# The first batch's second layer by seven products: right-hand sums made where the weights first stand, and one addition of the Fourier fold ahead of a subtraction

## The chip, the cores and the metric

The kernel runs on one core of one Trainium2 chip. The metric is the time of one execution on the device in microseconds (us); lower is better. All engines of the core (TensorE, VectorE, ScalarE, GpSimd, and SyncE, which issues most transfers) run their own queues of instructions in order and wait for each other by semaphores.

## The reference

Four batches of 8 heads of attention over 768 positions with 64 channels a head. A query sees a local window (distance under 16) and 24 block keys (the maximum of each 32 keys, with the blocks' mean values and log 32 added to the score). The heads are put side by side, x has 768 x 512 for each batch, and then:

```
X = np.fft.fft(x, axis=1)
X = np.fft.fft(X, axis=2)
mixed = np.real(X).astype(np.float32)
u = x + mixed
un = (u - mu) / np.sqrt(var + 1e-06)
ch = np.maximum(un @ w_ch1, 0.0) @ w_ch2
return (u + ch).astype(np.float32)
```

w_ch1 is 512 x 2048 and w_ch2 2048 x 512. Both come to the kernel as float64 and are turned into float32 on the chip.

## The kernel before

One program works through the four batches: attention of a batch, its Fourier transform as matrix products on folded halves (sums and differences of mirrored rows and columns, so that fewer products are needed), the layer norm, and the two layers. All products are float32 on TensorE. The order on each engine is the order in which a scheduler takes the Python program; `tc.issue_after(mark)` keeps a piece of work behind a marked instruction, and generators are driven in turn, so that the next batch's attention stands between the products of this batch's layers.

The layers are cut in two halves of the hidden channels, c = 0 and c = 1, four tiles of 256 hidden channels each (j, called weight tile 0 to 7). For a batch b the work runs: first layer of half 0 (`gen_hidden(b, 0)`), second layer of half 0 (`gen_out(b, 0)`), first layer of half 1, and then the second layer of half 1 beside the next batch's Fourier transform.

Products go by a scheme of seven in place of eight: a 2 x 2 block product needs seven products of sums of blocks (`A` blocks and left sums S1, S2, S3, S4; `B` blocks and right sums T1, T2, T3, T4). Each weight tile has seven parts: `_left_sums` or `_right_sums` makes parts 1 to 6 out of four blocks. T3 stands in the place of B12, so B12 is lost when T3 is made. Row tiles t (128 positions each) come in pairs i and i + 3; a pair's outcome is put together in three banks X, Y and Z of PSUM with a joining addition (`join`) after each product or two. PSUM gives four banks to this work (`bank`, a pool in turn) and four to the attention.

The weights of batch 0 are converted on the way (`convert`): raw words are loaded by SyncE (`load_raw`), VectorE masks exponent and mantissa (L1171, L1184), ScalarE does two steps (L1172, L1185), VectorE combines (L1187, L1189) and multiplies (through `tt`, whose additions and products all are recorded at L582). `gen_weights` goes through `plan`, a list of which weight tile is made when (first-layer tiles as (1, j), second-layer tiles as (2, j)), and each piece stands behind a stage's mark. A made tile is stored to DRAM (`dw1`, `dw2`) for the later batches, with its sums; the four second-layer tiles of half 0 were stored with their four blocks alone, batch 1 loaded these, made the sums between its first-layer products (`some_sums`) and stored them for batches 2 and 3.

In batch 0, half 0, the second layer goes without the seven products: six row tiles, each by eight plain products of 512 columns, L1730:

```
for n, j in enumerate(js):
    for hf in range(2):
        nc.tensor.matmul(ps, h[:, n, hf, P * t:P * (t + 1)], wt[2, b, j][:, 2 * hf:2 * hf + 2, :],
```

While they run, VectorE makes the weight tiles 3 of the second layer and 4, 5 and 6 of the first, and the attention of batch 1 goes on.

The fold of batch 0 (`mirror_halves`, `fold_channels`) runs on VectorE between the attention and the first transform (L1333): a mirror step makes sums and differences of mirrored columns (`zw`), then a channel step joins the two halves of the columns into `fg`.

Of the kernel before, what the change touches and what calls it, by code (L numbers as in the profile page):

```python
# [480 lines left out]
B11, T3, B21, B22, T1, T2, T4 = range(7)  # L481
A21, B12 = S3, T3
# [14 lines left out]
def _main_program(ctx, tc, q, k, v, moe_w_ch1, moe_w_ch2, out):  # L497
# [6 lines left out]
    NST = S // P  # L504
# [9 lines left out]
    HT = NST // 2  # L514
    HD = DM // 2
    NJ = NIT // 2
    NC = 4
# [63 lines left out]
    def tt(out, in0, in1, op):  # L581
        return nc.vector.tensor_tensor(out=out, in0=in0, in1=in1, op=op).ins  # L582
# [285 lines left out]
    def first_attention():  # L868

        x = x_of[0] = bpool.tile([P, NST, DM], FP, tag="x", bufs=2, name="x_0")  # L870
        fold = bpool.tile([P, 7, 2, S2], FP, tag="u", name="fold_0").rearrange("p a k n -> p (a k n)")
        wt["fold"] = split_fold(0, fold)
        turned = turned_to(0)
        for n in (1, 0):
            for e in range(2):
                turn(0, turned[0], n, e)
        for n in (1, 0):
            place(turned, n, 0, nc.scalar.copy)
            place(turned, n, 1, nc.vector.tensor_copy)
        key_maxima(0)  # L880
        load(0, 2)
        load_values(0, 1)
        load(0, 3)
        load_values(0, 2)
        ps, spread = {}, {}
        for g in range(-1, NP - 1):
            a, n = g + 1, g + 2
            ends = n == NP
            first = score_banks(a, 0)
            ps[a] = apool.tile([P, 2, NQ, QB], FP, tag="p", name=f"p_0_{a}")  # L890
            i = n - 1 if ends else g
            if i >= 0 and i not in spread:
                spread[i] = add_parts(i)
            wide_scores(a, 0, first)
            exponentials(ps[a], 0, first)
            if ends:
                spread_sums(n - 1, nc.scalar.copy, *spread[n - 1])
                mirror_halves(0, 0)
            elif g >= 0:
                spread_sums(g, nc.vector.tensor_copy, *spread[g])  # L900
            masks(ps[a], 0)
            second = score_banks(a, 1)
            if not ends:
                turned = turned_to(n)
                for i in ((1, 0), (1, 1), (0, 0), (0, 1))[:3 + (g < 0)]:
                    turn(n, turned[0], *i)
                place(turned, 1, 0, nc.scalar.copy)
                place(turned, 1, 1, nc.vector.tensor_copy if g < 0 else nc.scalar.copy)
                place(turned, 0, 0, nc.scalar.copy)
                if g < 0:  # L910
                    place(turned, 0, 1, nc.vector.tensor_copy)
                key_maxima(n % 2)
            wide_scores(a, 1, second)
            exponentials(ps[a], 1, second)
            masks(ps[a], 1)
            if g >= 0 and not ends:
                turn(n, turned[0], 0, 1)
                if g == 1:
                    spread[2] = add_parts(2)
                place(turned, 0, 1, nc.scalar.copy)  # L920
            if g >= 0:
                wide_values(0, g, ps[g], x)
            if g == 1:
                spread_sums(2, nc.scalar.copy, *spread[2])
            if g == 0:
                load_values(0, 3)
                load(1, 0)
                get_tables(0, lambda: load_raw(1))
                load_raw(2)
                block_sums(1, 0)  # L930
                load(1, 1)
                load_raw(4)
                fetch(out=sel, in_=dr["sel"].ap())
                fetch(out=near, in_=dr["near"].ap().rearrange("p (h i) c -> p h i c", h=2))
                fetch(out=half_of, in_=dr["half"].ap())
                fetch(out=mirror, in_=dr["mirror"].ap())
            for par in range(2 if g == 1 else 0):
                fold_sequence(par, 0, 2)
        mirror_halves(1, 0)
        fold_sequence(0, 2, 3)  # L940
        wide_values(0, NP - 1, ps[NP - 1], x)
        fold_sequence(1, 2, 3)
        load_values(1, 0)
        keep_busy(3, ps[NP - 1][:, 0].rearrange("p n c -> p (n c)"))
        nc.gpsimd.memset(zqs[0], 0.0)
        fold_sequence(0, 3, NP)
        mirror_halves(0, 1)
        fold_channels(0)
        fold_sequence(1, 3, NP)
        mirror_halves(1, 1)  # L950
        fold_channels(1)
# [3 lines left out]
        x, c = x_of[0], slice(P * g0, P * g1)  # L955
        tt(early[par][:, :, c], x[:, 0:HT, c], x[:, HT:NST, c], SUB if par else ADD)

    def mirror_halves(par, hi):

        Q, o = DM // 4, HD * hi  # L960
        sd, zw = early[par], wt["fold"][:, par]
        up, down = sd[:, :, o + 1:o + Q], sd[:, :, o + HD - 1:o + Q:-1]
        tt(zw[:, :, o + 1:o + Q], up, down, ADD)
        tt(zw[:, :, o + Q + 1:o + HD], up, down, SUB)

    def fold_channels(par):

        Q = DM // 4
        sd, zw, fg = early[par], wt["fold"][:, par], wt["fold"][:, 2 - 2 * par]
        edge = lambda c: (sd[:, :, c:c + 1], sd[:, :, HD + c:HD + c + 1])  # L970
        tt(fg[:, :, 0:1], *edge(0), ADD)
        tt(zqs[0][:, par, :, 0:1], *edge(Q), ADD)
        nc.gpsimd.memset(fg[:, :, Q:Q + 1], 0.0)
        plus, minus = (slice(o + 1, o + Q) for o in (0, Q))
        over, under = (slice(HD + o + 1, HD + o + Q) for o in (0, Q))
        tt(fg[:, :, plus], zw[:, :, plus], zw[:, :, over], ADD)
        tt(fg[:, :, minus], zw[:, :, minus], zw[:, :, under], ADD)
        tt(fg[:, :, HD:HD + 1], *edge(0), SUB)
        tt(fg[:, :, DM - 1:DM], *edge(Q), SUB)
        tt(fg[:, :, HD + 1:HD + Q], zw[:, :, minus], zw[:, :, under], SUB)  # L980
        marks["fold", 0] = tt(fg[:, :, HD + Q:DM - 1], zw[:, :, plus], zw[:, :, over], SUB)
# [214 lines left out]
    def make(f, j):  # L1196


        if f == 1:
            w = bpool.tile([P, 7, 2, P], FP, tag="w1", bufs=3, name=f"w1_0_{j}")  # L1200
            wv, to = w.rearrange("p a k n -> p a (k n)"), dw1[j].rearrange("p a k n -> p a (k n)")
        else:
            w = wv = bpool.tile([P, 7, HD], FP, tag="w2", bufs=NC, name=f"w2_0_{j}")
            to = dw2[j]
        yield from convert(pieces.index((f, j, 0)) // 2, wv[:, 0:4].rearrange("p a n -> p (a n)"))
        if f == 1:
            _left_sums(tt, wv)
        elif j < NC:

            to, wv = to[:, 0:4], wv[:, 0:4]  # L1210
        else:
            _right_sums(tt, wv)
        yield
        stores.append((to, wv))
        if len(stores) > 2 or len(pieces) == len(raws):
            fetch(out=stores[0][0], in_=stores.pop(0)[1])
        wt[f, 0, j] = w
        yield
# [20 lines left out]
        fetch(out=w, in_=dw1[j])  # L1239
        wt[1, b, j] = w  # L1240

    to_sum = []

    def some_sums(n):
        with tc.issue_after(marks["dense"]):
            for f, a in to_sum[:n]:
                f(*a)
        del to_sum[:n]

    def get_w2(b, j):  # L1250
        w = bpool.tile([P, 7, HD], FP, tag="w2", bufs=NC, name=f"w2_{b}_{j}")
        if b == 0:
            return
        wt[2, b, j] = w
        if b == 1 and j < NC:
            marks["load"] = fetch(out=w[:, 0:4], in_=dw2[j][:, 0:4])
            _right_sums(lambda *a: to_sum.append((tt, a)), w)
            to_sum.append((fetch, (dw2[j][:, 1:7], w[:, 1:7])))
        else:
            marks["load"] = fetch(out=w, in_=dw2[j])  # L1260


    tables = {}
# [177 lines left out]
    def gen_hidden(b, c):  # L1441
# [3 lines left out]
        for j in js:  # L1445
# [25 lines left out]
            nc.scalar.copy(out=c11, in_=X)  # L1471
            product(Y, A12, B21, True, True)
            marks["dense"] = tt(c11, Y, c11, ADD)
            some_sums(3 if (b, c) == (1, 0) and j else 0)
            yield
            product(X, S2_, T2, False, False)
            nc.scalar.copy(out=c12, in_=X)
            product(Z, S1, T1, True, False)
            nc.scalar.copy(out=c22, in_=Z)
            relu(c11)  # L1480
            some_sums(3 if (b, c) == (1, 0) and j else 0)
            yield
            product(X, S3, T3, False, False)
            marks["dense"] = tt(c22, X, c22, ADD)
            product(Z, S4, B22, False, True)
            marks["dense"] = tt(c12, Z, c12, ADD)
            some_sums(3 if (b, c) == (1, 0) and j else 0)
            yield
            product(X, A22, T4, False, True)
            nc.scalar.activation(out=c21, in_=X, func=AF.Relu)  # L1490
            relu(c22)
            relu(c12)
            issued.add(("h", b, j))
            some_sums(3 if (b, c) == (1, 0) and j else 0)
            yield

    H2 = S2 // 2
# [223 lines left out]
    def gen_out(b, c):  # L1721
        x, h = x_of[b], wt["h", b]
        js = range(NC * c, NC * (c + 1))
        if (b, c) == (0, 0):

            for t in range(NST):
                ps = bank([P, DM], f"o_{b}_{c}_{t}")
                for n, j in enumerate(js):
                    for hf in range(2):
# [2 lines left out]
                    if n % 2 == 0:  # L1732
                        yield
                tt(x[:, t, :], ps, x[:, t, :], ADD)
            issued.add(("o", b, c))
            return
        for i in range(HT):
            t1, t2 = slice(P * i, P * (i + 1)), slice(S2 + P * i, S2 + P * (i + 1))
            left = {A11: h[:, :, 0, t1], A12: h[:, :, 1, t1], A22: h[:, :, 1, t2]}
            for s in (S1, S2_, S3, S4):  # L1740
# [206 lines left out]
```

## Time and profile before

| what | value |
|---|---|
| time, median of 3 runs | 784.36 us (783.70 to 786.31) |
| the profiled execution | 782.39 us, span 780.6 us |
| granted TensorE clock | 0.999 |
| TensorE busy | 766.1 us, 98% of the span, 6020 products |
| VectorE busy | 534.4 us, 68% |
| ScalarE busy | 249.4 us, 32% |
| plain products of the first second layer | 96, from 126.8 to 173.4 us |

The span is the time from the first instruction to the last in the profiled execution. An engine's queue is in order, so an instruction that waits holds all behind it. In the rows of the timeline the first two numbers are the start and the busy time, and a bracket gives the idle time ahead of it and who ended it.

### The profile page before, as it was taken

The numbers are of one execution on the slowest core, as the hardware profiler recorded it, in microseconds if no ns is written. First come the engines' busy times: TensorE is split into PE (matmuls) and PEld (weight loads), VectorE is DVE, ScalarE is ACT, GpSimd is POOL, SyncE is SP. The second block draws the span as 40 slices with busy tenths as digits, with TensorE's granted clock in tenths as the row PEclk, the third lists the DMA queues.
The fourth block names the chain that finished last, engine by engine and source line by source line (L and its number), as shares of the span: only waits on it lengthen the run. The fifth ranks groups of instructions, "written<-read, shape, count | busy, mean of one in ns | idle before, by whom it ended". The sixth has DMA issues, their size and how long they took to land.

```text
span 780.6 us, 14876 instructions
## 1 busy us (share of the span) xinstructions
PE 766.1 (98%) x6020; PEld 578.0 (74%) x6020; DVE 534.4 (68%) x1123; ACT 249.4 (32%) x579; POOL 74.7 (10%) x102
## 2 busy tenths in 40 slices
PE   8999899999999999999999999999999999999997
PEld 5778555446598866787578866688669889889886
DVE  5789998777888556652758544553576887766762
ACT  4765656326536022100236012200126124104300
POOL 1001000000000030201210020300030004101500
PEclk9999999999999999999999999999999999999999
DMA  9998979696855179986342169720624143204001
GB/s 203 259 240 163 217 253 302 178 280 175 245 141 157 37 214 219 248 124 182 128 166 96 55 209 197 200 81 1 255 63 143 41 181 143 95 1 188 1 29 57
DMA packets 135900, 120.35 MB, mean 154 GB/s; under 512 B 94512, under 2 KB 117392, under 8 KB 135824
## 3 DMA queue, kind: packets, MB, share of 16 engines
q1 hardware_dynamic: 134672, 117.05, 54.9%
q0 software_dynamic: 576, 2.10, 0.7%
q8 instruction: 49, 0.80, 0.5%
q10 hardware_dynamic: 576, 0.17, 0.1%
q14 instruction: 27, 0.22, 0.1%
HBM read 95.71 MB, written 23.59 MB: 153 GB/s over the span
## 4 chain that ended last, share of the span: by engine, by line
PE 81%; DVE 9%; DMA 5%; ACT 3%; issue 1%; SPq 1%; POOL 0%; DVEq 0%; ACTq 0%; POOLq 0%
PE ox L1753 18%; PE hx L1460 13%; PE oz L1753 9%; PE hz L1460 6%; PE o L1730 5%; PE oy L1753 4%; PE t L1633 4%; DMA words<-in_moe_w_ch_dram 3%; PE hy L1460 3%; PE y L1333 2%; PE f L1633 2%; PE mx L1292 2%; PE sc L810 2%; PE av L846 1%; DVE w L582 1%
## 5 line engine op out<-in xcount | busy, mean ns | idle before, releaser
L1460 PE MATMUL hx<-u,w 128*128 128x384 f32 x384 | 140.0, 492 | 0.5 <-ACT h L1471 0.3
L1460 PEld LDWEIGHTS hx<-u,w 128*128 128x128 f32 x384 | 70.9, 190 | 52.8 <-ACT p L817 3.7
L1753 PE MATMUL oz<-w,s 128*128 128x256 f32 x336 | 81.7, 380 | 0.0
L1753 PE MATMUL ox<-w,s 128*128 128x256 f32 x336 | 80.1, 380 | 0.2 <-DVE s L582 0.2
L1753 PE MATMUL ox<-w,h 128*128 128x256 f32 x336 | 79.6, 381 | 0.0
L1753 PEld LDWEIGHTS ox<-w,h 128*128 128x128 f32 x336 | 63.0, 190 | 10.7 <-issue 1.2
L1460 PE MATMUL hz<-u,w 128*128 128x384 f32 x192 | 70.4, 487 | 0.4 <-DVE u L582 0.4
L582 DVE TENSOR_TENSOR x<-ox,x 128x256 f32<-128x256 f32 x84 | 35.5, 423 | 51.2 <-PE ox L1753 50.8
L1753 PEld LDWEIGHTS ox<-w,s 128*128 128x128 f32 x336 | 63.0, 190 | 9.6 <-DVE s L582 0.6
L1753 PEld LDWEIGHTS oz<-w,s 128*128 128x128 f32 x336 | 63.2, 190 | 9.0 <-DVE x L582 0.4
L1460 PEld LDWEIGHTS hz<-u,w 128*128 128x128 f32 x192 | 36.2, 190 | 25.7 <-DVE u L582 1.0
L1471 ACT COPY h<-hx 128x384 f32<-128x384 f32 x24 | 11.5, 478 | 118.7 <-PE hx L1460 118.7
L1730 PE MATMUL o<-w,h 128*128 128x512 f32 x96 | 42.2, 595 | 0.9 <-DVE w L582 0.9
L1753 PE MATMUL oy<-w,h 128*128 128x256 f32 x168 | 40.7, 381 | 0.7 <-ACT h L1682 0.7
L1636 ACT COPY f<-t 128x192 f32<-128x192 f32 x52 | 15.8, 303 | 78.3 <-PE t L1633 78.1
L1612 POOL TENSOR_SCALAR h<-h 128x768 f32<-128x768 f32 x12 | 25.4, 2128 | 137.6 <-DVE h L1592 137.6
L585 POOL TENSOR_TENSOR vb<-vb 96x512 f32<-96x512 f32 (+2 forms) x20 | 20.4, 1024 | 182.5 <-DMA vb<-in_v_dram 115.8
L1460 PE MATMUL hy<-u,w 128*128 128x384 f32 x96 | 35.2, 488 | 1.5 <-DVE h L582 1.5
L582 DVE TENSOR_TENSOR x<-oz,x 128x256 f32<-128x256 f32 x42 | 17.8, 423 | 26.7 <-PE oz L1753 26.4
L1753 PEld LDWEIGHTS oy<-w,h 128*128 128x128 f32 x168 | 31.5, 190 | 5.9 <-ACT h L1682 1.5
L1730 PEld LDWEIGHTS o<-w,h 128*128 128x128 f32 x96 | 18.0, 190 | 23.8 <-issue 21.2
L1490 ACT ACTIVATE h<-hx 128x384 f32<-128x384 f32 x24 | 11.7, 489 | 62.2 <-PE hx L1460 62.2
(236 smaller groups left out, 1327.4 us busy)
## 6 DMA issues: line engine op xcount, KB each, us to landing
w<-dw SPq DMA_DIRECT2D x42, 896.0 KB, 5.8
words<-in_moe_w_ch_dram SPq DMA_DIRECT2D x32, 512.0 KB, 5.8
dw<-w SPq DMA_DIRECT2D x12, 896.0 KB, 7.8
vw<-in_v_dram SPq DMA_DIRECT2D x47, 192.0 KB, 5.6
out_dram<-x SPq DMA_DIRECT2D x23, 256.0 KB, 2.0
vb<-in_v_dram SPq DMA_DIRECT2D x24, 192.0 KB, 6.9
kn<-in_k_dram SPq DMA_DIRECT2D x9, 384.0 KB, 5.9
qn<-in_q_dram SPq DMA_DIRECT2D x9, 384.0 KB, 7.0
```

The source lines that it names most:

```text
L582: return nc.vector.tensor_tensor(out=out, in0=in0, in1=in1, op=op).ins
L585: return nc.gpsimd.tensor_tensor(out=out, in0=in0, in1=in1, op=op).ins
L810: ins = nc.tensor.matmul(ps[h][r:r + 64, i, :], kt[rows, o:o + 64], qt[rows, o:o + BLOCK], start=True, stop=True)
L1292: nc.tensor.matmul(out, y[:, g], table, start=False, stop=True, skip_group_check=True)
L1333: nc.tensor.matmul(y, fgs[b][par][:, st, P * g:P * (g + 1)], fs[par][:, g % 2, st, :], start=(st == 0), stop=(st == n - 1))
L1460: ins = nc.tensor.matmul(ps, w[:, a, kk, :], u[:, r, kk, :], start=start and kk == 0, stop=stop and kk == 1, skip_group_check=True)
L1490: nc.scalar.activation(out=c21, in_=X, func=AF.Relu)
L1612: nc.gpsimd.tensor_scalar(out=t, in0=t, scalar1=0.0, scalar2=None, op0=ALU.max)
L1633: marks["two"] = nc.tensor.matmul(o, left(j, a, m), rhs(r, m), start=m in (1, 5), stop=m in (2, 3, 4, 5, 7), skip_group_check=True).ins
L1636: nc.scalar.copy(out={1: f[:, 0], 6: f[:, 1], 7: g}[m], in_=t)
L1730: nc.tensor.matmul(ps, h[:, n, hf, P * t:P * (t + 1)], wt[2, b, j][:, 2 * hf:2 * hf + 2, :], start=(n, hf) == (0, 0), stop=(n, hf) == (NC ...
L1753: nc.tensor.matmul(ps, left[a][:, n, :], wt[2, b, j][:, r, :], start=start and n == 0, stop=stop and n == NC - 1, skip_group_check=True)
```

## The change

Four edits.

The second layer of batch 0, half 0: the row tiles 0 and 3 stay plain. The pairs of tiles 1 and 4, and 2 and 5, go by seven products of 256 columns, with four left sums (128 x 512) and seven joins (128 x 256) a pair. Ahead of tile 0 stand T1, T2 and T4 of weight tiles 0 and 1, ahead of tile 3 those of weight tiles 2 and 3; behind tile 3 stand the four T3 and the stores of parts 1 to 6.

The making of these four weight tiles stores part 0 alone (128 KB in place of 512). Batch 1 loads all seven parts (896 KB in place of 512), and its twelve sums and four stores of 768 KB go.

In the fold of batch 0, one mirror step is cut in two: its addition stays, its subtraction moves into `fold_channels(0)`, behind the first of the joining additions there.

```diff
-        mirror_halves(0, 1)
+        mirror_halves(0, 1, ADD)
         fold_channels(0)
...
         tt(fg[:, :, plus], zw[:, :, plus], zw[:, :, over], ADD)
+        if par == 0:
+            mirror_halves(0, 1, SUB)
         tt(fg[:, :, minus], zw[:, :, minus], zw[:, :, under], ADD)
...
-            to, wv = to[:, 0:4], wv[:, 0:4]
+            to, wv = to[:, 0:1], wv[:, 0:1]
...
-        if b == 1 and j < NC:
-            marks["load"] = fetch(out=w[:, 0:4], in_=dw2[j][:, 0:4])
-            _right_sums(lambda *a: to_sum.append((tt, a)), w)
-            to_sum.append((fetch, (dw2[j][:, 1:7], w[:, 1:7])))
-        else:
-            marks["load"] = fetch(out=w, in_=dw2[j])
+        marks["load"] = fetch(out=w, in_=dw2[j])
...
-            some_sums(3 if (b, c) == (1, 0) and j else 0)
...
-        if (b, c) == (0, 0):
-
-            for t in range(NST):
+        plain = (0, HT) if (b, c) == (0, 0) else ()
+        if plain:
+            for t in plain:
+                for j in js[0:2] if t == 0 else js[2:4]:
+                    w = wt[2, 0, j]
+                    tt(w[:, T1], w[:, B12], w[:, B11], SUB)
+                    tt(w[:, T2], w[:, B22], w[:, T1], SUB)
+                    tt(w[:, T4], w[:, B21], w[:, T2], SUB)
                 ps = bank([P, DM], f"o_{b}_{c}_{t}")
...
                 tt(x[:, t, :], ps, x[:, t, :], ADD)
-            issued.add(("o", b, c))
-            return
-        for i in range(HT):
+            for j in js:
+                w = wt[2, 0, j]
+                tt(w[:, T3], w[:, B22], w[:, B12], SUB)
+                fetch(out=dw2[j][:, 1:7], in_=w[:, 1:7])
+        for i in range(1 if plain else 0, HT):
```

What this moves on the engines. First TensorE, around the scores of batch 1's last pair of heads in the second layer of half 0. Names: `ss` are the scores against block keys, `o_0_4` and `o_0_5` the banks of plain row tiles 4 and 5, `hx` the next first layer. Before:

```order
L828 MATMUL ss_3_1779<-qt_3_1554,km_83 32x384 x4
L1730 MATMUL o_0_4_1721<-w_0_1_1382,h_0_1255 128x512 x2
L1730 MATMUL o_0_4_1721<-w_0_2_1415,h_0_1255 128x512 x2
L1730 MATMUL o_0_4_1721<-w_0_3_1504,h_0_1255 128x512 x2
L1730 MATMUL o_0_5_1796<-w_0_0_1250,h_0_1255 128x512 x2
L1730 MATMUL o_0_5_1796<-w_0_1_1382,h_0_1255 128x512 x2
L1730 MATMUL o_0_5_1796<-w_0_2_1415,h_0_1255 128x512 x2
L1730 MATMUL o_0_5_1796<-w_0_3_1504,h_0_1255 128x512 x2
L1460 MATMUL hx_4_1809<-u_816,w_0_4_1538 128x384 x2
```

Now, at the same scores (`ox_0_1` and `oz_0_1` are banks X and Z of pair 1, `ox_0_2` is X of pair 2, `qk` the transposes of the next head, `s_0_0_1` the left sums of pair 1):

```order
L828 MATMUL ss_3_1843<-qt_3_1554,km_83 32x384 x4
L710 MATMUL qk_0_0_1912<-ident,kn_0_1233 128x128 x3
L710 MATMUL qk_0_1_1918<-ident,kn_0_1233 128x128 x3
L710 MATMUL qk_0_0_1924<-ident,qn_0_1235 128x128 x3
L710 MATMUL qk_0_1_1930<-ident,qn_0_1235 128x128 x3
L834 MATMUL vs_3_1937<-vbs_1_1237,sel 128x64
L1746 MATMUL ox_0_2_1775<-w_0_0_1250,h_0_1255 128x256
L1746 MATMUL ox_0_1_1728<-w_0_0_1250,s_0_0_1_1721 128x256
L1746 MATMUL ox_0_1_1728<-w_0_1_1382,s_0_0_1_1721 128x256
```

The transposes stand ahead of the second layer's remaining products. The first product of pair 2 takes the bank that plain tile 3 had, so it waits for the join of tile 3; the next one adds to bank X of pair 1 again and waits for that bank's first join.

Then VectorE, at the end of the conversion of weight tile 6. Names: `w_0_6` is that tile, `words` the raw words, `x_145` batch 0's rows, `x_919` batch 1's, `rec` the attention's reciprocals. Before:

```order
L582 TENSOR_TENSOR w_0_6_1620<-w_0_6_1620,words 128x1024
L1171 TENSOR_SCALAR words<-words 128x1024
L582 TENSOR_TENSOR x_919<-av_2_1_1635,rec 128x2x3x64
L582 TENSOR_TENSOR w_0_6_1620<-w_0_6_1620 128x256
L582 TENSOR_TENSOR x_145<-o_0_1_1617,x_145 128x512
L582 TENSOR_TENSOR w_0_6_1620<-w_0_6_1620 128x2x256
L582 TENSOR_TENSOR x_145<-o_0_2_1700,x_145 128x512
L582 TENSOR_TENSOR w_0_6_1620<-w_0_6_1620 128x256
L582 TENSOR_TENSOR x_145<-o_0_3_1711,x_145 128x512
```

Now:

```order
L582 TENSOR_TENSOR w_0_6_1632<-w_0_6_1632,words 128x1024
L582 TENSOR_TENSOR x_919<-av_2_0_1646,rec 128x2x3x64
L856 RECIPROCAL rec<-av_2_1_1647 128x6
L582 TENSOR_TENSOR w_0_6_1632<-w_0_6_1632 128x256
L582 TENSOR_TENSOR x_919<-av_2_1_1647,rec 128x2x3x64
L582 TENSOR_TENSOR w_0_6_1632<-w_0_6_1632 128x2x256
L582 TENSOR_TENSOR x_145<-o_0_3_1629,x_145 128x512
L582 TENSOR_TENSOR w_0_6_1632<-w_0_6_1632 128x256
L582 TENSOR_TENSOR w_0_3_1504<-w_0_3_1504 128x256
L582 TENSOR_TENSOR x_145<-ox_0_1_1728,x_145 128x256
L582 TENSOR_TENSOR x_145<-oz_0_1_1730,x_145 128x256
L582 TENSOR_TENSOR x_145<-oy_0_1_1729,x_145 128x256
```

Where the joins of plain tiles 1, 2 and 3 stood between the last sums of weight tile 6, there now stand the join of plain tile 3, the T3 of weight tile 3 and the first joins of pair 1's X, Z and Y. The conversions of weight tiles 4, 5 and 6 stand ahead of them in both.

Last VectorE in the fold of batch 0, after the attention of the last heads. Before:

```order
L582 TENSOR_TENSOR wide<-x_145 128x3x128 x2
L582 TENSOR_TENSOR fold_146<-wide 128x3x127 x2
L582 TENSOR_TENSOR fold_146<-wide 128x3 x2
L582 TENSOR_TENSOR fold_146<-fold_146 128x3x127 x2
L582 TENSOR_TENSOR fold_146<-wide 128x3 x2
L582 TENSOR_TENSOR fold_146<-fold_146 128x3x127 x2
```

Now:

```order
L582 TENSOR_TENSOR wide<-x_145 128x3x128 x2
L582 TENSOR_TENSOR fold_146<-wide 128x3x127
L582 TENSOR_TENSOR fold_146<-wide 128x3 x2
L582 TENSOR_TENSOR fold_146<-fold_146 128x3x127
L582 TENSOR_TENSOR fold_146<-wide 128x3x127
L582 TENSOR_TENSOR fold_146<-fold_146 128x3x127
L582 TENSOR_TENSOR fold_146<-wide 128x3 x2
L582 TENSOR_TENSOR fold_146<-fold_146 128x3x127 x2
```

One operation of 128 x 3 x 127 from `wide` (the mirror subtraction) now stands behind the first `fold`-from-`fold` addition.

More of the change, by code (lines that the diff above doesn't have):

```diff
@@ L956, in fold_sequence, with mirror_halves @@
         tt(early[par][:, :, c], x[:, 0:HT, c], x[:, HT:NST, c], SUB if par else ADD)
-    def mirror_halves(par, hi):
+    def mirror_halves(par, hi, *ops):
         Q, o = DM // 4, HD * hi
@@ L962, in mirror_halves @@
         up, down = sd[:, :, o + 1:o + Q], sd[:, :, o + HD - 1:o + Q:-1]
-        tt(zw[:, :, o + 1:o + Q], up, down, ADD)
-        tt(zw[:, :, o + Q + 1:o + HD], up, down, SUB)
+        for op in ops or (ADD, SUB):
+            at = o + (Q if op is SUB else 0)
+            tt(zw[:, :, at + 1:at + Q], up, down, op)
     def fold_channels(par):
@@ L1240, in get_w1 @@
         wt[1, b, j] = w
[L1242 to L1248, printed above, removed]
     def get_w2(b, j):
@@ L1480, in gen_hidden @@
             relu(c11)
-            some_sums(3 if (b, c) == (1, 0) and j else 0)
             yield
@@ L1486, in gen_hidden @@
             marks["dense"] = tt(c12, Z, c12, ADD)
-            some_sums(3 if (b, c) == (1, 0) and j else 0)
             yield
@@ L1493, in gen_hidden @@
             issued.add(("h", b, j))
-            some_sums(3 if (b, c) == (1, 0) and j else 0)
             yield
```

## The prediction

> **What bounds the kernel now.** I read the page first: busy time of each engine, then the chain that ended last.
>
> ```profile
> PE 766.1 (98%) x6020; PEld 578.0 (74%) x6020; DVE 534.4 (68%) x1123; ACT 249.4 (32%) x579; POOL 74.7 (10%) x102
> ...
> PE 81%; DVE 9%; DMA 5%; ACT 3%; issue 1%; SPq 1%; POOL 0%; DVEq 0%; ACTq 0%; POOLq 0%
> ```
>
> TensorE is busy for 98% of the span and carries 81% of the chain. Work taken off it is worth its full time, if nothing new makes it wait. So I asked what it waits for: over the whole span (three of the rows), and after 174 us (first and last of five rows).
>
> ```profile
> PE o L1730 <- DVE w L582: 0.9, 1, 0.9
> PE mx L1374 <- ACT big L1338: 0.7, 1, 0.7
> PE y L1333 <- DVE fold L582: 0.6, 1, 0.6
> ```
> ```profile
> PE oy L1753 <- ACT h L1682: 0.7, 2, 0.3
> ...
> PE y L1333 <- PE oz L1753: 0.2, 1, 0.2
> ```
>
> After 174 us the five add up to 1.6 us: a delay given to TensorE before that is hardly won back later. Then the busy time of the engines by stage (columns PE, PEld, DVE, ACT, POOL, clock, DMA share, GB/s):
>
> ```profile
> 126.50:174.00 47.50, 46.60 (x311) 21.72 (x310) 35.72 (x49) 16.70 (x23) 0.00 (x0) 1.00 0.83 249
> 174.00:230.00 56.00, 55.30 (x312) 37.19 (x312) 47.68 (x77) 28.44 (x61) 0.74 (x1) 1.00 0.69 196
> ```
>
> The first row is the stage of the change, the first second layer: TensorE is full, VectorE has 11.8 us free. The timeline of TensorE in it:
>
> ```profile
> 126.75 6.17 PE L1730 MATMUL o<-w,h 128*128 128x512 f32 x14
> 133.83 6.28 PE L1730 MATMUL o<-w,h 128*128 128x512 f32 x14 [0.90 <-DVE w L582]
> 140.03 1.20 PE L846 MATMUL av<-vw,p 64*32 64x65 f32 x96
> 141.16 0.94 PE L851 MATMUL av<-vs,p 64*128 64x130 f32 x12
> 142.03 17.43 PE L1730 MATMUL o<-w,h 128*128 128x512 f32 x40
> 159.40 1.60 PE L810 MATMUL sc<-qt,kt 64*64 64x32 f32 x96
> 160.93 0.85 PE L828 MATMUL ss<-qt,km 64*32 64x384 f32 x8
> 161.71 12.29 PE L1730 MATMUL o<-w,h 128*128 128x512 f32 x28
> 173.83 1.45 PE L1460 MATMUL hx<-u,w 128*128 128x384 f32 x4
> ...
> 178.99 0.82 PE L710 MATMUL qk<-ident,kn 128*128 128x128 f32 x6
> ...
> 180.30 1.46 PE L1460 MATMUL hx<-u,w 128*128 128x384 f32 x4
> 181.59 0.33 PE L834 MATMUL vs<-vbs,sel 96*128 96x64 f32 x2
> ```
>
> And VectorE's (an instruction's pitch is the distance to the next start):
>
> ```profile
> 135.85 0.69 DVE L582 TENSOR_TENSOR x<-o,x 128x512 f32<-128x512 f32 x1 [2.08 <-PE o L1730]
> 136.46 0.68 DVE L1171 TENSOR_SCALAR words<-words 128x1024 int32<-128x1024 int32 x1
> 137.06 0.69 DVE L1184 TENSOR_SCALAR w<-words 128x1024 int32<-128x1024 int32 x1
> 142.13 0.27 DVE L856 RECIPROCAL rec<-av 128x6 f32<-128x6 f32 x2 [4.39 <-PE av L851]
> 142.32 1.19 DVE L1187 SCALAR_TENSOR_TENSOR words<-words 128x1024 int32<-128x1024 int32 x1
> 143.42 1.22 DVE L1189 SCALAR_TENSOR_TENSOR w<-words,w 128x1024 f32<-128x1024 uint32 x1
> ...
> 159.03 0.40 DVE L582 TENSOR_TENSOR w<-w 128x256 f32<-128x256 f32 x1
> 159.36 0.67 DVE L582 TENSOR_TENSOR x<-o,x 128x512 f32<-128x512 f32 x1
> 159.96 0.67 DVE L582 TENSOR_TENSOR w<-w 128x512 f32<-128x512 f32 x1
> ...
> 162.09 1.01 DVE L582 TENSOR_TENSOR p<-p,near 128x384 f32<-128x384 f32 x2
> ```
>
> The row to see is 159.36: tile 1's joining addition, whose last product ended near 142.03 + 2 x 0.43 = 142.9, runs 16 us later. From 142.32 on VectorE works without a gap through three tiles of weights, in its queue's order, and the joins stand behind them. Before the change nobody needs that join early: with four banks it is asked for only by the plain tiles far behind it.
>
> **The products.** An instruction of 512 columns has a pitch of (159.40 - 142.03) / 40 = 0.434 us; a tile is 16 of them, 6.9 us. Those of 256 columns, later in the trace:
>
> ```profile
> 265.21 1.89 PE L1753 MATMUL oz<-w,s 128*128 128x256 f32 x8
> 266.94 1.89 PE L1753 MATMUL ox<-w,s 128*128 128x256 f32 x8
> ```
>
> Eight take 1.73 us. A pair is 56 of these by seven products, 12.1 us, against 64's worth, 13.8: 1.73 us saved, 3.45 for two pairs. That is the gain, all of it on TensorE's path.
>
> **The walk.** By the order, TensorE does nine of the plain products (two instructions, 0.87 each), then waits for weight tile 3, then seven more, the attention values, X, Y and Z of pair 1 (24 instructions), the scores, the next head's transposes (before, these stood inside the next hidden layer), and then asks for a bank that tile 3's join must empty first. On the profile's clock:
>
> TensorE: 126.75 + 9 x 0.87 = 134.5. Weight tile 3 was ready at 133.83 (TensorE's start above); five new 256-wide subtractions stand ahead of it, at (159.36 - 159.03) = 0.33: 135.5, or 134.5 at best if gaps of VectorE take them. Then 7 x 0.865 + 2.0 (140.03 to 142.03) = 143.55; 24 x 0.216 = 5.2 makes 148.75; scores 2.3 (159.40 to 161.71) makes 151.05; transposes 1.3 and 0.3 make 152.7. There it asks.
>
> VectorE: from 135.5, seven subtractions 2.35, tile 0's join 0.6, two T3 0.67, five left sums of 512 columns 5 x 0.6, one more T3 0.33, two conversion steps 1.2, a reciprocal 0.1: 143.75, by when the values it needs (143.55) are there. Then the 24 rows from 142.32 through the join at 159.36, 17.64 us in the trace (to 159.96), with the 512-wide subtraction and a reciprocal now ahead of the join, 0.7: 162.1. There tile 3's join is done.
>
> So TensorE waits 162.1 - 152.7 = 9.4 us, a wait not in the trace of before. One quarter-product aside, the next product needs X's own join, three 0.33-us rows behind: 163.1. The 43 quarter-products left take 43 x 0.432 = 18.6: 181.65. Among them S3 x T3 waits once more: VectorE has two joins 0.67, a left sum 0.6, the two masks 1.0 (162.09), a conversion step 1.1 and the join 0.33 to do, 166.8, where TensorE comes at 165.7: 1.1. The next hidden layer starts at 182.75. Before it started at 173.83, and its 1.6 us of transposes came after: 175.45. **Loss in this stage: 7.3 us**, the 3.45 saved already in it.
>
> **The clock after the wait.** The only long idle of TensorE in the trace is the start:
>
> ```profile
> 1.40 3.78 PE L1805 MATMUL warm<-zeros 128*128 128x512 f32 x4 [1.40 <-POOL zeros L1802]
> 5.05 1.51 PE L728 MATMUL qk<-ident,kn 128*128 128x128 f32 x6
> ```
> ```profile
> PEclk9999999999999999999999999999999999999999
> ```
>
> Four 512-wide take 3.65 us, 0.91 each against 0.434 later, and six transposes 1.51 against 0.82 (178.99): half rate from 1.40 to about 6.5, 5.1 us, 2.5 us lost. After 9.4 us of standing idle I take the same: of the 2.5 the wait for X's join hides 0.4 and the second wait 1.1, so **1.0** is left; bounds 0 and 2.5. The Trainium skill ("TensorE: Matmul & The Clock Gate", Part 1) has the array's clock halved after an idle window of about 3.4 us and restored after as long a busy one; by it 1.7 us would be lost and 0.2 left. The start agrees with the halving, though for 5.1 us, and no run so far shows an idle inside the program long enough to try the rest.
>
> **The fold.** The mirror subtraction moves behind the "plus" addition that TensorE waits for:
>
> ```profile
> 43.82 1.01 DVE L582 TENSOR_TENSOR fold<-fold 128x381 f32<-128x381 f32 x2
> 44.75 0.23 DVE L582 TENSOR_TENSOR fold<-wide 128x3 f32<-128x3 f32 x2
> ```
>
> Two of 381 columns take 0.93, so the transform that waited 0.6 starts 0.47 sooner; the later wait of 0.7 for a copy may shrink as well. A later wait for something else can swallow both: 0 to 1.2, taken 0.5.
>
> **Moved and removed work.** The twelve sums of batch 1, and its four stores, leave the stage from about 290 us; its loads grow from 512 to 896 KB. TensorE waits there for none of them: nothing, covered by TensorE. In the stage itself the stores grow by 4 x (768 + 128 - 512) = 1.5 MB while the DMA share is 0.83:
>
> ```profile
> words<-in_moe_w_ch_dram SPq DMA_DIRECT2D x32, 512.0 KB, 5.8
> dw<-w SPq DMA_DIRECT2D x12, 896.0 KB, 7.8
> ```
>
> One of them, tile 3's, waits on SyncE's queue for T3 (VectorE, right behind the late join) and holds the raw words of the last first-layer tile behind it; those tiles have some 8 us of slack, VectorE's free 56 - 47.7 in 174 to 230. If a load slips by the difference of a store's and a load's landing, 2.0 us may show: 0 to 2.0, taken 0.
>
> **Sum.** 7.3 + 1.0 - 0.5 = 7.8 us. The profiled execution took 782.39 (span 780.6), so 790.2 there; the median of 784.36 is 2.0 above the profiled one, and with the same offset the forecast is **792.2**. Low: weight tile 3 at 134.5 (-1.0), second wait gone (-1.1), clock kept (-1.0), fold 1.2 (-0.7): +4.0, 788.4. High: clock 1.5 more, a late load 2.0, no fold gain 0.5: +11.8, 796.2.
>
> **Rivals.**
> The clock stays full through the wait: 6.8 net, 791.2. For it: the PEclk row reads 9 even in the slice of the slow start. Against: the durations there. 0.30.
> The raw words come late and the second half's weights are what TensorE waits for, too: 794 to 796.2. For: the DMA share. Against: the slack. 0.13.
> The change is faster: VectorE's order does not bind, tile 3's join is done by 152.7 instead of 162.1, and the products' saving is left: -3.45 - 0.5, 780.4. It needs 9.4 us of the 18.3 us ahead of the join to be gone, or the join to run ahead of the conversions. VectorE has 11.8 us free in the stage, but before 142, while it waits for the values; from 142.32 on it has none. 0.05.
> The wait is there and is given back, or is half as long: within 0.3% (2.35 us, about what a measurement of this kernel can tell from no change). Against: 1.6 us of waits are all there is to give back after 174. 0.04.
> The forecast keeps 0.48. Slower by over 0.3%: 0.48 + 0.30 + 0.13 = 0.91. The range from 788.4 to 796.2 leaves out the last two, and some of the tail above.
>
> **What would show it.** Right: in TensorE's waits a new first row, the 256-wide second-layer line waiting for an addition on VectorE, 8 to 11 us once, between 150 and 165; a join of tile 3 that runs some 12 us after its product ended, behind the third weight tile's sums; the next hidden layer's start near 183; 32 512-wide instructions at L1730's successor in place of 96; matmuls right behind the wait at about twice their pitch (else the clock rival). The first transform of the fold about 0.5 sooner. Wrong: that wait under 5 us, or with the next hidden layer ahead of 176 the gain is real; a wait of like size for weights in 185 to 230 would be the rival of the loads; and any time below 784.

## The result and the profile after

The changed kernel takes 791.73 us (median of 7 runs, 789.58 to 794.12), the kernel before 783.70 in the same comparisons (781.66 to 786.31): a ratio of 1.0109, interval 1.0084 to 1.0133, slower by about 8 us. The profiled execution took 794.12 us, its span is 792.3.

The first and the fourth part of its page, engines and chain, against those of before:

```profile
PE 767.6 (97%) x6068; PEld 591.0 (75%) x6068; DVE 541.1 (68%) x1145; ACT 248.9 (31%) x579; POOL 74.3 (9%) x102
...
PE 80%; DVE 12%; ACT 3%; DMA 2%; issue 1%; SPq 0%; DVEq 0%
```

Two things are seen at once. TensorE's busy time has not fallen by 3.45 us but risen by 1.5, although it does less, so something ran slower. And VectorE's share of the chain went from 9 to 12%. TensorE's waits over the span name the place (the first two rows, and the wait for weight tile 3):

```profile
PE ox L1746 <- DVE x L582: 4.1, 1, 4.1
PE qk L710 <- ACT p L829: 3.6, 1, 3.6
...
PE o L1721 <- DVE w L582: 0.6, 1, 0.6
```

The timeline of TensorE from the start of the second layer to the next first layer:

```profile
131.53 7.89 PE L1721 MATMUL o<-w,h 128*128 128x512 f32 x18
139.99 4.56 PE L1721 MATMUL o<-w,h 128*128 128x512 f32 x10 [0.57 <-DVE w L582]
...
151.75 1.89 PE L1746 MATMUL oz<-w,s 128*128 128x256 f32 x8
153.57 1.60 PE L810 MATMUL sc<-qt,kt 64*64 64x32 f32 x96
...
156.53 0.55 PE L710 MATMUL qk<-ident,kn 128*128 128x128 f32 x3
160.68 0.90 PE L710 MATMUL qk<-ident,kn 128*128 128x128 f32 x3 [3.60 <-ACT p L829]
...
163.72 0.69 PE L834 MATMUL vs<-vbs,sel 96*128 96x64 f32 x2
168.55 1.22 PE L1746 MATMUL ox<-w,h 128*128 128x256 f32 x2 [4.13 <-DVE x L582]
169.56 3.44 PE L1746 MATMUL ox<-w,s 128*128 128x256 f32 x8
172.84 1.03 PE L1746 MATMUL oz<-w,s 128*128 128x256 f32 x4
...
189.67 1.45 PE L1450 MATMUL hx<-u,w 128*128 128x384 f32 x4
```

Between Z's last products (151.75) and bank X's next ones (169.56) lie 16 us, for 4.4 us of work by the durations of before: the scores 2.3, the transposes 1.6, and one quarter-product. Eight instructions then take 3.44 us, where eight of the same shape take 1.89 at 151.75. And behind the first wait (160.68) three transposes take 0.90 us, the three ahead of it 0.55. The row of the clock on the page shows the place: the 6 is the slice from 158 to 178 us, the 8 the start of the program, and before the row has a 9 throughout.

```profile
PEclk8999999969999999999999999999999999999999
```

VectorE at the end of the wait: the last words' mask, tile 3's join, the first join of bank X.

```profile
164.13 0.69 DVE L1174 TENSOR_SCALAR words<-words 128x1024 int32<-128x1024 int32 x1 [1.86 <-DMA words<-in_moe_w_ch_dram]
...
167.81 0.69 DVE L582 TENSOR_TENSOR x<-o,x 128x512 f32<-128x512 f32 x1
...
169.07 0.42 DVE L582 TENSOR_TENSOR x<-ox,x 128x256 f32<-128x256 f32 x1
```

TensorE started 0.74 us after tile 3's join did. In this execution the join also stood behind 1.86 us of waiting for raw words.

The wait of 3.6 us that is put down to ScalarE has the same origin. Two conversion steps stand ahead of the block score's exponentials in ScalarE's queue: ScalarE was idle for 2.08 us until VectorE had masked the words, did both steps from 158.16, and came to the exponentials at 160.16, though the scores had ended near 156.5.

The stage by windows, first before, from the first plain product to the next first layer, then after (columns as in the prediction):

```profile
126.75:173.83 47.08, 46.18 (x310) 21.42 (x308) 35.30 (x49) 16.45 (x23) 0.00 (x0) 1.00 0.82 249
```
```profile
131.53:189.67 58.14, 48.92 (x371) 34.12 (x370) 46.91 (x79) 20.54 (x34) 0.00 (x0) 0.88 0.77 235
```

The stage is 11.1 us longer; the 1.6 us of transposes that it now holds are missing behind it. From the first plain product to the next batch's Fourier transform it is 93.91 us before (126.75 to 220.66) and 103.54 after (131.53 to 235.07), a loss of 9.6. Batch 1's second layer of half 0 gives 2.4 back. Values of the attention there before:

```profile
348.37 0.33 PE L834 MATMUL vs<-vbs,sel 96*128 96x64 f32 x2
348.63 0.54 PE L846 MATMUL av<-vw,p 64*32 64x65 f32 x24
349.11 2.86 PE L1753 MATMUL ox<-w,h 128*128 128x256 f32 x12
351.89 0.88 PE L846 MATMUL av<-vw,p 64*32 64x65 f32 x48
352.71 0.93 PE L851 MATMUL av<-vs,p 64*128 64x130 f32 x6
353.57 1.13 PE L1753 MATMUL ox<-w,h 128*128 128x256 f32 x4
354.63 0.54 PE L846 MATMUL av<-vw,p 64*32 64x65 f32 x24
355.11 0.93 PE L851 MATMUL av<-vs,p 64*128 64x130 f32 x6
355.97 1.99 PE L1753 MATMUL oy<-w,h 128*128 128x256 f32 x8
```

and after:

```profile
362.09 0.33 PE L834 MATMUL vs<-vbs,sel 96*128 96x64 f32 x2
362.35 1.20 PE L846 MATMUL av<-vw,p 64*32 64x65 f32 x96
363.48 0.94 PE L851 MATMUL av<-vs,p 64*128 64x130 f32 x12
364.35 3.72 PE L1746 MATMUL ox<-w,h 128*128 128x256 f32 x16
```

The same attention stands in three pieces between the products before, and in one after. Before it takes 355.97 - 348.37 = 7.60 us with 16 product instructions of 0.216 in it, so 4.1 without them; after 364.35 - 362.09 = 2.26. That is 1.9 of the 2.4 us; 0.2 more is a wait for a left sum at 324.83 in the kernel before, and the rest is not traced. No engine waits in the rows above: the waits don't show them, only the timeline does.

The rest of the 11.7 us between the two spans lies ahead of the stage: the first transform starts at 48.66 in place of 44.42. In a second profile of the same kernel (below) it starts at 45.59.

### The profile page after: what moved, and what is told of

Read it like the earlier page. It is cut to its first block, busy times and chain, and to the rows that moved or that the text cites. A ratio compares the mean times of both kernels' runs of the same rounds, so it can differ in the third digit from the quotient of the medians.

```text
span 792.3 us, 14996 instructions
## 1 busy us (share of the span) xinstructions
PE 767.6 (97%) x6068; PEld 591.0 (75%) x6068; DVE 541.1 (68%) x1145; ACT 248.9 (31%) x579; POOL 74.3 (9%) x102
## 4 chain that ended last, share of the span: by engine, by line
PE 80%; DVE 12%; ACT 3%; DMA 2%; issue 1%; SPq 0%; DVEq 0%
PE ox L1746 19%; PE hx L1450 13%; PE oz L1746 10%; PE hz L1450 6%; PE oy L1746 5%; PE t L1619 4%; PE hy L1450 3%; PE y L1323 3%; DVE w L582 2%; PE f L1619 2%; PE mx L1282 2%; DMA words<-in_moe_w_ch_dram 2%; PE sc L810 2%; DVE w L1192 2%; PE sc L750 1%
## 5 line engine op out<-in xcount | busy, mean ns | idle before, releaser
L1746 PE MATMUL ox<-w,h 128*128 128x256 f32 x368 | 87.5, 382 | 4.1 <-DVE x L582 4.1
L1746 PE MATMUL ox<-w,s 128*128 128x256 f32 x368 | 89.3, 385 | 0.0
L1746 PE MATMUL oz<-w,s 128*128 128x256 f32 x368 | 89.0, 380 | 0.0
L1746 PEld LDWEIGHTS ox<-w,h 128*128 128x128 f32 x368 | 69.5, 191 | 16.1 <-DVE x L582 4.3
L1746 PEld LDWEIGHTS ox<-w,s 128*128 128x128 f32 x368 | 70.2, 193 | 10.6 <-DVE x L582 0.8
L582 DVE TENSOR_TENSOR x<-ox,x 128x256 f32<-128x256 f32 x92 | 38.9, 423 | 56.3 <-PE ox L1746 56.0
L1746 PEld LDWEIGHTS oz<-w,s 128*128 128x128 f32 x368 | 69.6, 190 | 9.5 <-DVE x L582 0.4
L1746 PE MATMUL oy<-w,h 128*128 128x256 f32 x184 | 44.3, 381 | 0.7 <-ACT h L1668 0.7
L582 DVE TENSOR_TENSOR s<-h 128x512 f32<-128x512 f32 x46 | 31.4, 682 | 0.9 <-ACT h L1458 0.6
L1477 ACT ACTIVATE h<-hx 128x384 f32<-128x384 f32 x24 | 11.7, 489 | 61.9 <-PE hx L1450 61.9
L582 DVE TENSOR_TENSOR h<-hy,h 128x384 f32<-128x384 f32 x24 | 13.3, 556 | 25.7 <-PE hy L1450 25.6
```

The lines of the kernel that those rows point to most:

```text
L1746: nc.tensor.matmul(ps, left[a][:, n, :], wt[2, b, j][:, r, :], start=start and n == 0, stop=stop and n == NC - 1, skip_group_check=True)
```

## The experiments

Times are medians with the kernel before timed on the same chip; ratios with 95% intervals. All leave the computation as it is, except for products that nobody reads or that add zero, where that is said.

**The fold's edit alone**, on the kernel before.

```diff
-        mirror_halves(0, 1)
+        mirror_halves(0, 1, ADD)
...
+        if par == 0:
+            mirror_halves(0, 1, SUB)
```

> The kernel before with the fold's edit alone. In the profile of the changed kernel the first transform starts 0.5 us sooner, but the first second layer starts no sooner. Theory (the gain is swallowed on the way by waits for ScalarE and VectorE): within 0.3 us of before. Rival (the gain stays on TensorE's path): 0.5 us faster, and the first second layer starts 0.5 us sooner against the first transposes.

784.14 us against 783.59, ratio 1.0017 (0.9996 to 1.0038). The query transposes and the first transform, before:

```profile
42.99 0.82 PE L710 MATMUL qk<-ident,qn 128*128 128x128 f32 x6
44.42 1.58 PE L1333 MATMUL y<-fs,fold 128*128 128x193 f32 x8 [0.61 <-DVE fold L582]
```

and with the edit:

```profile
45.12 0.82 PE L710 MATMUL qk<-ident,qn 128*128 128x128 f32 x6
46.08 1.71 PE L1336 MATMUL y<-fs,fold 128*128 128x193 f32 x8
```

The transform follows the transposes after 0.96 us in place of 1.43: the edit does what it says. From that transform to the first plain product it is 82.37 us against 82.33, so up to there the gain lasted in this profile, contrary to the theory. By the next batch's Fourier transform it is gone: from the query transposes 177.72 us (45.12 to 222.84) against 177.67 (42.99 to 220.66). The time shows nothing of it, and a gain of that size is below what these runs can tell.

**The storing alone**, on the kernel before.

```diff
-            to, wv = to[:, 0:4], wv[:, 0:4]
+            to, wv = to[:, 0:1], wv[:, 0:1]
...
                 tt(x[:, t, :], ps, x[:, t, :], ADD)
+            for j in js:
+                _right_sums(tt, wt[2, 0, j])
+                fetch(out=dw2[j][:, 1:7], in_=wt[2, 0, j][:, 1:7])
```

(and batch 1 loads all seven parts, without its sums).

> The kernel before, all six row tiles plain, but the right-hand sums of the four weight tiles are made and stored behind the first second layer, and batch 1 makes none. Theory (TensorE's queue in batch 1's second layer keeps the attention values in one piece when the twelve sums are gone, as its order shows, and that is worth 2.4 us): 1.5 to 2.5 us faster than before, about 781.5, less what the twelve sums cost where they are now made. Rival (that 2.4 us came from elsewhere): no change, within 0.7 us.

781.36 us, ratio 0.9968 (0.9951 to 0.9984): 2.2 us faster. Batch 1's second layer takes 43.50 us (321.38 to 364.88) against 45.93 before, and its attention values stand in one piece:

```profile
348.70 0.33 PE L834 MATMUL vs<-vbs,sel 96*128 96x64 f32 x2
348.96 1.20 PE L846 MATMUL av<-vw,p 64*32 64x65 f32 x96
350.09 0.94 PE L851 MATMUL av<-vs,p 64*128 64x130 f32 x12
```

All kernels here that make no sums in batch 1 have 43.5 us there, and the three that do 45.6 to 45.9. In batch 0, where the sums are now made, it is 94.61 us from the first plain product to the next batch's Fourier transform in place of 93.91.

**The seven products alone**: the changed kernel, with weights stored and summed as before.

```diff
-            to, wv = to[:, 0:1], wv[:, 0:1]
+            to, wv = to[:, 0:4], wv[:, 0:4]
...
                 tt(w[:, T3], w[:, B22], w[:, B12], SUB)
-                fetch(out=dw2[j][:, 1:7], in_=w[:, 1:7])
```

> The changed kernel with its seven products, but batch 1 makes and stores the right-hand sums as before. Theory (the loss is the wait for tile 3's join, the wait for a block score's exponentials and the slow clock behind them, 9.4 us in that stage; the removed sums give 2.4 back): 9 to 10 us slower than before, 2 us slower than the changed kernel. Rival (the larger stores and loads of the changed kernel cost the time): as before or faster, under 784.

791.37 us, ratio 1.0097 (1.0062 to 1.0131). The loss is the seven products', not that of the larger stores and loads. But it was to be 2 us above the changed kernel and is level with it. Its waits (rows of TensorE):

```profile
PE ox L1762 <- DVE x L582: 5.3, 1, 5.3
...
PE vs L834 <- ACT kt L713: 2.8, 1, 2.8
```

The stage takes 55.04 us, 3.1 less than in the changed kernel, and VectorE never waits for raw words in it. In both profiles of the changed kernel it does, for 1.9 and 3.0 us. So the larger stores may lengthen the wait by about what batch 1 gives back; that is argued from these profiles, and the next kernel but one speaks against it in part.

**The joins first.** The changed kernel, with joins, T3 and the left sums of pair 2 put ahead in VectorE's queue. The same work, other order.

```diff
-                tt(x[:, t, :], ps, x[:, t, :], ADD)
+                with tc.high_priority(300):
+                    tt(x[:, t, :], ps, x[:, t, :], ADD)
...
+                with tc.high_priority(300) if (b, c) == (0, 0) else ExitStack():
+                    marks["dense"] = tt(*a)
```

(and the same around T3 and pair 2's left sums).

> The changed kernel with the joins of the first second layer, the four T3 and the left sums of pair 2 ahead of the weights' conversions in VectorE's queue; the same work in all. Theory (the order of VectorE's queue makes the wait): the waits of 4.1 and 3.6 us and the slow clock go, 3.45 us of products and 2.4 us of batch 1 are gained against before: 777 to 780. Rival (VectorE has too much work in this stage, in whatever order): the wait moves to a sum or to a weight tile of the next first layer, 787 to 791.

781.31 us, ratio 0.9972 (0.9954 to 0.9990): 10 us faster than the changed kernel. The one wait left in the stage, the product behind it, and the stage by windows:

```profile
151.28 1.99 PE L1749 MATMUL ox<-w,s 128*128 128x256 f32 x8 [1.01 <-DVE x L582]
```
```profile
130.44:175.01 44.57, 43.44 (x357) 30.30 (x356) 43.24 (x76) 14.64 (x22) 0.00 (x0) 1.00 0.91 272
```

Tile 3's join starts 148.74 - 130.44 = 18.3 us after the first plain product, where it started 36.3 us after it in the changed kernel. The order of VectorE's queue makes the wait; the amount of work does not. (TensorE's order moved with it: the scores stand later, at 163.94, and the transposes are back in the next first layer.) Yet the last row shows how near the limit is: VectorE is busy for 43.24 of 44.57 us.

The stage is 2.5 us shorter than before, but up to the next Fourier transform only 1.0 us is left of it (92.87 against 93.91), and so the time misses the expected 777 to 780. Of the other 1.5 us, 1.4 are waits for ScalarE's copies in the next first layer, 1.7 us in place of 0.3 before (second row; no run removes them):

```profile
PE av L846 <- issue: 3.3, 1, 3.3
PE hx L1450 <- ACT h L1461: 1.7, 2, 0.9
```

The first row is a stop ahead of the stage, at attention values near 77 us, for which the profile shows no cause. The profiles have it there in other lengths, 0.7 us in the changed kernel, 1.2 with the storing alone, 3.0 with the seven products alone, and none before. So the start of the stage can't be compared between single profiles.

**Tile 3's join alone first**: only the first of these edits.

> The changed kernel with the join of plain tile 3 alone ahead in VectorE's queue (behind weight tile 4's first steps). Theory (the whole group of joins stands behind the conversions, and X's first join is next): TensorE gets four quarter-products of pair 2 earlier, then waits for the join of bank X at the same place; the wait is named after the next product and 1.3 us shorter, the time 1 to 2 us under the changed kernel, about 790. Rival (the bank of tile 3 is the only thing that is late): the wait goes, 780 to 783.

789.14 us, ratio 1.0058 (1.0033 to 1.0082). The waits:

```profile
PE ss L828 <- ACT p L817: 2.3, 1, 2.3
PE ox L1747 <- DVE x L582: 2.2, 1, 2.2
```

The wait for bank X's join is next, as the theory said, not gone. Tile 3's join now starts at 149.11, bank X's first one at 165.83. The wait is shorter than in the changed kernel by 1.9 us, not by 1.3, and VectorE does not wait for raw words here, though the stores are the changed kernel's. So the stores alone don't decide that.

**TensorE kept busy, first try.** Sixteen products with a zero operand are added into bank Z behind S1 x T1.

```diff
             product(Z, S1, T1, True, False)
+            if (b, c, i) == (0, 0, 1):
+                for _ in range(16):
+                    nc.tensor.matmul(Z[0:32], nothing, wt[2, b, 0][:, 0, :], start=False, stop=False, skip_group_check=True)
```

> The changed kernel with 16 products of a zero operand (32 columns of weights, 256 wide, 7 us at full clock) added into bank Z behind pair 1's S1 x T1, which change no value. They fill the time in which TensorE waits. Theory (standing idle halves the clock, which costs 2.1 us behind the wait): the products behind the wait run at 0.22 us each and the time is 1.5 to 2.5 us under the changed kernel, about 789.5, though 7 us of work were added. Rival (those products are slow for another reason, or the added work comes on top): as the changed kernel or slower.

791.93 us, ratio 1.0099 (1.0075 to 1.0123): inconclusive. Rows of its timeline:

```profile
148.56 7.09 PE L1765 MATMUL oz<-w,nothing 128*32 128x256 f32 x32
...
162.82 1.50 PE L828 MATMUL ss<-qt,km 64*32 64x384 f32 x8 [5.63 <-DVE rec L856]
...
168.08 1.89 PE L1746 MATMUL ox<-w,s 128*128 128x256 f32 x8
```

They stand ahead of the scores, not in the wait, so an idle stretch of 5.6 us was left and the whole came 3 us later. The slow clock fell on the transposes, and the products at 168.08 were at full speed.

**TensorE kept busy, second try.** Six products into a bank nobody reads, behind the transposes.

```diff
+        if (b, g) == (2, 0):
+            ps = abank([P, S2], "busy")
+            for _ in range(6):
+                nc.tensor.matmul(ps, ident, qn[:, 0, 0:3, :].rearrange("p j n -> p (j n)"), start=True, stop=True)
```

> The changed kernel with six more products (ident by a query tile, 384 wide, into a bank of their own that nobody reads) behind the transposes in the second layer, so that TensorE works in the 4 to 5 us ahead of tile 3's join instead of standing idle. It adds 3.9 us of work at full clock. Theory (the idle time halves the clock and the products behind it lose 2.1 to 2.6 us): the 256-wide products behind the wait run at 0.22 us each, the stage takes 55.5 to 58 us in place of 58.1 and 60.1, the time is about 2 us under the changed kernel, 789 to 790. Rival (the products behind the wait are slow for another reason, or the join itself is what sets the end): stage and time as in the changed kernel, 791 to 793.

789.31 us, against 782.55 for the kernel before on the chip of this run, ratio 1.0087 (1.0069 to 1.0106). Rows of its timeline:

```profile
159.14 6.83 PE L717 MATMUL busy<-qn,ident 128*128 128x384 f32 x12
...
165.98 1.51 PE L1750 MATMUL ox<-w,h 128*128 128x256 f32 x6
167.34 1.89 PE L1750 MATMUL ox<-w,s 128*128 128x256 f32 x8
...
185.03 1.45 PE L1454 MATMUL hx<-u,w 128*128 128x384 f32 x4
```

The products behind the wait run at full speed: 44 quarter-products take 185.03 - 165.98 = 19.05 us, as 44 x 0.432 = 19.0 says. In the changed kernel the same 44 took 189.67 - 168.55 = 21.1, in its second profile 21.9. So the slow products come of TensorE's standing idle, and they cost 2.1 to 2.9 us. Whether the added 3.9 us of work brought the time down is not shown: it is 6.8 us above the kernel before, where the changed kernel was 8.0 above it, but the intervals of the two ratios overlap. The stage, at 58.02 us, is no shorter than the 58.14 of the first profile: the join came later in it (raw words 2.58 us late), and the added products ended some 1.2 us behind the join.

**The joins first, with the old fold.**

```diff
-        mirror_halves(0, 1, ADD)
+        mirror_halves(0, 1)
...
-        if par == 0:
-            mirror_halves(0, 1, SUB)
```

> The kernel with the joins first, but the fold as before. Theory (the fold's edit gives nothing): as with the joins first, 781.3 within 1 us. Rival (the edit's 0.5 us counts there): 0.5 us slower.

780.48 us, ratio 0.9962 (0.9945 to 0.9978), within 1 us of the kernel with the new fold: the fold's edit can't be told here either. Of all kernels this has the lowest median, 3.65 us under 784.13 of the kernel before beside it; by the intervals it is not told from the storing alone.

**The changed kernel once more.**

> The changed kernel once more, for a second profile. Theory (the 4.8 us by which the first second layer starts later than in the profile of before belong to that one execution): another value of that start, between 127 and 132 us, and again about 58 us from there to the next first layer. Rival (the change makes the start later): 131.5 us again.

793.87 us, one run. The first transform starts at 45.59 (48.66 in the first profile, 44.42 before), the first plain product at 130.16, and the next first layer at 190.22: 60.1 us of stage. So the late start of the first transform belongs to the execution; in the other kernels' profiles it lies between 43.58 and 46.08. The first plain product is 3.4 us later than before, and 2.2 of them arise between that transform and it. The waits of the stage come again (5.3 and 3.6 us); the stage is 2 us longer than the expected 58, with raw words 3.0 us late.

## Why the prediction was right, and where its terms were not

Forecast 792.2, measured 791.73, and the likeliest case was the one that came about. Point by point:

The mechanism held: a new wait for tile 3's join, behind the conversions. TensorE went on 37.0 us after the first plain product (168.55 - 131.53); the walk had tile 3's join done at 162.1 - 126.75 = 35.35, and the 1.86 us of late raw words are of the size of the difference. The kernel with the joins first shows the cause by removing it.

The wait came in two rows, 3.6 us for a block score's exponentials on ScalarE and 4.1 for the join, where the walk had 9.4 in one: the transposes stood ahead of the wait in the walk, and in the run nine of the twelve stood behind its first part. It changes nothing at the end, since the join comes last.

The second wait, at S3 x T3, taken at 1.1, did not come. The slow clock took its place: 2.1 to 2.9 us, all of it visible, against 1.0 taken; the bound of 2.5 was nearly right. The Trainium skill's time for a restart, about 3.4 us ("TensorE: Matmul & The Clock Gate", Part 1), would have given 1.7, an estimate below both measurements. The rival with a chance of 0.30, that the clock stays full, is refuted by the granted clock of 0.88 in the stage; the time alone could not have refuted it, since its 791.2 lies as near 791.73 as the forecast does.

The late raw words were taken at 0, with a bound of 2.0: 1.9 and 3.0 us in the two profiles, inside the wait for the join and not, as the rival had it, at the second half's weights.

So the stage was mis-sized: 9.6 us up to the next Fourier transform (10.9 in the second profile), where 7.3 + 1.0 had been taken.

The step that failed outright is "The twelve sums of batch 1 ... TensorE waits there for none of them: nothing". That argument looked at waits only. Without the sums batch 1's second layer is 2.4 us shorter, which the storing alone shows; 1.9 of them are in the attention values, which the scheduler now puts in one piece. The order of TensorE's instructions of both kernels has this difference, at a place that the walk did not cover.

The fold's 0.5 us was there at the first transform (1.43 - 0.96) and can't be told in the time.

The sum came out right partly because these errors cancel: +1.3 to +2.6 in the stage, -2.4 in batch 1. That it is within 0.5 us of the measured time is luck.

The rival of the faster side needed the join by 152.7. Its price of 780.4 is where the kernel with the joins first arrived, at 781.31, by another sum: 2.4 of that comes from batch 1.

## What to carry to other kernels

Where a change makes a bank's release urgent, look up what stands ahead of the release in its engine's queue, instruction by instruction: here 18 us of work that was in no hurry stood ahead of 0.6 us that was. A change that saves products and adds additions moves the bound towards the engine of the additions; the same work in another order made a loss of 8 us into a gain of 2. That gain is no larger than the storing's alone (781.31 and 781.36): what the seven products save here does not show in the time. And work that leaves a place with no wait in it still moves what is scheduled there: compare the orders of the whole program, not only around the change.

## What the runs showed of the hardware that I had not expected

The length of a wait alone does not tell whether the clock slows behind it. Behind 1.01 us (joins first) eight products took 1.99 us, near the usual 1.89. In the kernel with tile 3's join first, 2.27 us were enough:

```profile
154.02 1.60 PE L810 MATMUL sc<-qt,kt 64*64 64x32 f32 x96
157.89 1.51 PE L828 MATMUL ss<-qt,km 64*32 64x384 f32 x8 [2.27 <-ACT p L817]
```

Block scores of 1.51 us are those that take 0.85 elsewhere. In the second profile of the changed kernel 1.49 us were enough, in a first layer:

```profile
98.23 2.38 PE L1450 MATMUL hy<-u,w 128*128 128x384 f32 x4 [1.49 <-DVE h L582]
```

The same four products behind the same wait of 1.49 us take 1.56 us in the kernel before (at 97.05) and in the first profile of the changed kernel (at 101.30). Scores of 64 x 64 x 32 stand ahead of both of these short waits; whether they count as idle, no run here tells. Another stop slowed the products, too: behind the 3.26 us ahead of the stage, in the kernel with the joins first, twelve groups of 64 x 130 take 1.67 us in place of 0.94.

An attention value's groups among 256-wide products cost more than by themselves: six of 64 x 130 have 0.93 us there and twelve 0.94 in one piece. Why that is so, no run here tells.
